# Attention, routed experts and a gated layer on one core: compact attention state, keys transposed in scaled form, two banks for y, ten row buffers, and only the needed zones zeroed

## The chip, the cores and the metric

One core of one Trainium2 chip runs the whole program. The metric is the device time of one launch in microseconds (us). The engines are TensorE (PE in the rows, PEld for its weight loads), VectorE (DVE), ScalarE (ACT), GpSimd (POOL) and SyncE (SP, which issues most transfers).

## The reference, cut to what matters

```python
def _attn_ref(r, k, v, w, u):          # B, H, S, D = 4, 8, 768, 48
    state = zeros((B, H, D, D))
    for t in range(S):
        cur = einsum('bhd,bhe->bhde', u * k[t], v[t])
        y[t] = einsum('bhd,bhde->bhe', r[t], state + cur)
        state = w[:, :, None] * state + einsum('bhd,bhe->bhde', k[t], v[t])

x = y.transpose(0, 2, 1, 3).reshape(3072, 384)
logits = x @ w_gate + modality_bias[modality_id]        # 8 experts
e_idx = argmax(logits); gate_w = softmax(logits)[e_idx]
x = gate_w * (relu(x @ w1[e_idx]) @ w2[e_idx])          # w1 384x1024, w2 1024x384
xn = x / rms(x) * rms_g
out = (silu(xn @ w_gate2) * (xn @ w_val)) @ w_out       # 384 -> 1536 -> 384
```

All data are float32.

## The kernel before, in words

**Attention.** The sequence is cut into 24 tiles of 128 tokens of one batch (tile i: chunk i // 4, batch i % 4), worked on in a software pipeline of steps `s_`. In step s the code issues, in this order:

- `a_state(s-2)`: VectorE adds the state product of tile s-2 (a PSUM bank, `s`) to the state `St` of its batch (L782), GpSimd multiplies the sum by the decay (L784), each in two halves of 64 partitions.
- `a_T(s+1)`, `a_scale(s+1)`: TensorE transposes r and k of the next tile, VectorE scales both transposes by powers of w out of PSUM (L726, `rT` and `kT`).
- `a_load(s+4)`: three loads of 192 KB by SyncE. The rings hold 4 tiles of r, 4 of k and 6 of v.
- `a_A(s)`, `a_mask(s)`: scores on TensorE, the causal copy on VectorE.
- `a_Y(s-1)`: y of tile s-1, from the state (L755) and from the masked scores (L759), in one bank (4), copied out by ScalarE (L762); then the state product (L767).
- `a_diag(s+2)`, `a_rk(s+3)`, `a_kp(s+3)`: products of r, k and u; keys scaled for the state (`kpad`), both on GpSimd; 8 diagonal tiles on ScalarE (L711).
- `hard()`, `send_one()`: routing, and the scatter of one finished tile of x to its experts' rows in `xs` (L242, GpSimd).
- `a_X(s-2)`: gate logits and x of tile s-2 (L656). ScalarE copies x into a buffer of a ring of 6 (L660), GpSimd writes the token number beside it (L661); in the next step VectorE reads the logits (L668).

**Routing.** Every three tiles a route of about 17 small VectorE operations is started. It advances by one operation at each call of `soft()`, which the attention code makes between its own VectorE operations; `hard()` runs what is left up to the rank matmuls (L355, L356, bank 7).

**Experts.** `xs` has for each expert a zone of 800 rows ahead of its tokens, and one dummy zone. A slot is 792 rows of one expert. Slots that are not full read into the zone. `zero_rows` writes zeros to all nine zones during attention (L257, 1.2 MB each, on SyncE's queue, from step 3 to step 19). Two slots known to be full start early, before the last tiles are scattered; the others (two fixed ones, `NFIX`, and more in a loop that is rarely entered) come from a table that is ready at sub-step 9 of the expert phase. The expert phase is a list of sub-steps k of 18 matmuls each (L611, L629 to L631), fed by weight loads of SyncE (L541, L543) through a ring of three chunks.

**The gated layer** follows, from about 455 us on, and is not touched.

Within attention and the expert phase the order of each engine's instructions is that of the code. Every engine works its queue in order, and so does SyncE with its transfers.

Of the kernel before, what the change touches and what calls it, by code (L numbers as in the profile page):

```python
# [18 lines left out]
NP = H // 2  # L19
# [20 lines left out]
XW = DM + 2  # L40
G = 3
EARLY_T = 15
NEARLY = 2
# [13 lines left out]
def moe_chain_kernel(ctx: ExitStack, tc: tile.TileContext, r, k, v, w, u, mod, wgate, mbias,  # L57
# [13 lines left out]
    def bank(n, name=None):  # L71
        return ps.tile([128, 512], F32, tag=f"b{n}", name=name or f"b{n}")
# [19 lines left out]
    def pad_tile(nm, n, pool):  # L92
        if pool is cst:
            t = room[:, 3 * n + "rkv".index(nm), :].rearrange("p (h d) -> p h d", h=H)
        else:
            t = pool.tile([128, H, 64], F32, name=f"{nm}pad{n}")
        pads[nm, n] = t
        P.memset(t[:, :, D:64], 0.0)

# [147 lines left out]
    def body(fast):  # L247
        with ExitStack() as st:
            moe = ExitStack()
            mp = moe.enter_context(tc.tile_pool(name="mp", bufs=2))  # L250
            zrow = {}

            def zero_rows(e):
                if not zrow:
                    zrow[0] = tabs[0:ZONE // 10, KD * HALF:KD * HALF + XW]
                    P.memset(zrow[0], 0.0)
                d = SP.dma_start(out=xs[e * STRIDE:e * STRIDE + ZONE, :].rearrange("(p t) d -> p t d", t=10),  # L257
                                 in_=zrow[0].rearrange("p (t d) -> p t d", t=1).to_broadcast([ZONE // 10, 10, XW]))
                if e < E:
                    tc.declare_no_dep(d.ins, group="xs", reason="rows that no token has")  # L260
                    tc.add_to_no_dep_group("xs", d.ins)

# [49 lines left out]
            def route(g, ls, xt):  # L312
# [39 lines left out]
                yield HARD  # L352
                bk = bank(7, "rank")
                rk = bk[:, 0:G * E]
                T.matmul(rk, tri16, M.rearrange("p g e -> p (g e)"), start=True, stop=False)  # L355
                T.matmul(rk, ones16, C[:, 0:G, :].rearrange("p g e -> p (g e)"), start=False, stop=True)  # L356
                if (g + 1) * G in (EARLY_T, NT):
                    T.matmul(bk[0:1, 128:128 + E], ones16[:, 0:1], C[:, G, :], start=True, stop=True)
                yield SOFT
# [11 lines left out]
                if (g + 1) * G in (EARLY_T, NT):  # L371
                    cnt = p.tile([1, E], F32, name="cntf")
                    V.tensor_copy(cnt, bk[0:1, 128:128 + E])
# [275 lines left out]
            yt, xt, ls = {}, {}, {}  # L649

            def a_X(i):

                yT = yt.pop(i)
                xb = bank(6, "xb")
                for q in range(NP):
                    T.matmul(xb[:, q * SW:(q + 1) * SW], yT[:, q, :], selw[:, q, :], start=True, stop=True)  # L656
                xb3 = xb[:, 0:NP * SW].rearrange("p (q n) -> p q n", q=NP)
                if fast:
                    x = xt[i] = ap.tile([128, XW], F32, name="x", bufs=6)
                    A.activation(x[:, 0:DM].rearrange("p (q n) -> p q n", q=NP), xb3[:, :, 0:2 * D], AF.Copy)  # L660
                    P.tensor_copy(x[:, DM + 1:XW], tokid[:, i:i + 1])  # L661
                g, o = divmod(i, G)
                if o == 0:
                    ls[g] = ap.tile([128, G, E], F32, name="ls", bufs=3)
                return ls[g][:, o, :], xb3[:, :, 2 * D:SW].rearrange("p q e -> p e q")
# [5 lines left out]
            if fast:  # L671
                ac = at.enter_context(tc.tile_pool(name="ac", bufs=1, side="right"))
                kpad = [ac.tile([128, H, 64], F32, name=f"kp{n}") for n in range(5)]
                St = [ac.tile([128, H, 64], F32, name=f"St{b}") for b in range(B)]

# [9 lines left out]
                def padded(nm, i):  # L685
                    return pads[nm, i % ring[nm]]
# [6 lines left out]
                def a_kp(i):  # L693
                    if i < 5:
                        P.memset(kpad[i][:, :, D:64], 0.0)
                    P.tensor_tensor(kpad[i % 5][:, :, 0:D], padded("k", i)[:, :, 0:D], Qt, op=ALU.mult)
                    if i < B:
                        P.memset(St[i], 0.0)

# [46 lines left out]
                def a_Y(i):  # L746
# [16 lines left out]
                    if c < NC - 1:  # L763
                        sb[i] = bank(5, "s")
                        for q in range(NP):
                            for hf in range(2):
                                T.matmul(sb[i][64 * hf:64 * hf + 64, q * D:(q + 1) * D], kpad[i % 5][:, 2 * q + hf, :],  # L767
                                         vv[:, 2 * q + hf, 0:D], start=True, stop=True, skip_group_check=True)

                def a_state(i):  # L770
                    if i in sb:
                        b = i % B
                        sp = sb.pop(i)[:, 0:NP * D].rearrange("p (q d) -> p q d", q=NP)
                        decay = PT[:, :, 128:129].to_broadcast([128, NP, D])
                        for n in range(2):
                            rows = slice(64 * n, 64 * n + 64)
                            sf = St[b].rearrange("p (q two) d -> p two q d", two=2)[rows, n, :, 0:D]
                            if i < B:
                                V.tensor_tensor(sf, sp[rows], decay[rows], op=ALU.mult)
                            else:  # L780
                                tmp = ap.tile([128, NP, D], F32, name=f"stmp{n}")[rows]
                                V.tensor_tensor(tmp, sp[rows], sf, op=ALU.add)  # L782
                                soft()
                                P.tensor_tensor(sf, tmp, decay[rows], op=ALU.mult)  # L784
            else:
                def a_row(i):
                    t = xt[i] = ap.tile([128, XW], F32, name="x", bufs=6)
                    P.tensor_copy(t[:, DM + 1:XW], tokid[:, i:i + 1])
# [18 lines left out]
            with tc.manual_schedule(engines={ET.PE, ET.DVE, ET.Activation, ET.Pool, ET.SP}) if fast else nullcontext():  # L807
# [25 lines left out]
                for s_ in range(0 if fast else -1, NT + 2):  # L833
                    if s_ == 3:
                        zero_rows(E)
                    if 5 <= s_ < 5 + 2 * E and s_ % 2:
                        zero_rows((s_ - 5) // 2)
                    if fast:
# [42 lines left out]
                    if s_ == NT:  # L881
                        for kk in range(KD):
                            slot_x(slots[0], 0, kk, bank((0, 1, 5)[kk], "xtp"))
                    if s_ == 1:
# [85 lines left out]
            for k in range(len(steps) + 1):  # L970
# [52 lines left out]
                if k == NROUTE:  # L1023
# [45 lines left out]
            def overflow():  # L1069
                nonlocal mp, raws1, raws2, xrows  # L1070
                with tc.tile_pool(name="mo", bufs=2) as mp:
                    raws1, raws2, xrows = slot_memory()
                    with tc.For_i(NFIX, ncount, 1) as jv:
                        un = unit_new(slot_new(rt["tabR"], jv), (0, 1))
                        slot_rows(un.s)
                        unit_weights(un, range(1))
# [210 lines left out]
```

## Time and profile before

| | |
|---|---|
| three runs | 914.93, 905.68, 906.70 us; median 906.7 |
| the profiled execution | 903.63 us, span 901.8 us |
| TensorE, VectorE, ScalarE, GpSimd busy | 92%, 53%, 37%, 30% of the span |
| attention | from the start to about 190 us |
| expert phase | first matmul at 195.07 us, to about 445 us |
| gated layer | about 455 us to the end |

Time is read by stage: in the stretch that the change touches, the question is which wait ends last. A line of a view tells when an instruction started, how long it took, and in brackets how long its engine stood idle before it and what ended that.

### The profile page before, as it was taken

Reading aid. Unit: us, or ns where it says so; the run is one execution under the profiler, and the core shown is the slowest. Engines: PE = TensorE matmul, PEld = TensorE weight load, DVE = VectorE, ACT = ScalarE, POOL = GpSimd, SP = SyncE. Lnnn points to the kernel's source line nnn. Section 1 sums busy time; section 2 is a strip of 40 time slices with the busy share of each in tenths; the row PEclk is TensorE's granted clock in tenths of the full one; section 3 lists DMA queues with packets and bytes.
Section 4 is the critical chain, followed back from the end, with each engine's and each line's share of the span. In section 5 each row is a group of like instructions: output and inputs, shape, how many; then the busy total and the mean of one; then the engine's idle time right before and its main releaser. Section 6 shows DMA issues by size and latency. Waiting matters only on the chain.

```text
span 901.8 us, 13427 instructions
## 1 busy us (share of the span) xinstructions
PE 828.4 (92%) x5097; PEld 751.5 (83%) x5097; DVE 478.5 (53%) x969; ACT 332.8 (37%) x731; POOL 267.5 (30%) x314
## 2 busy tenths in 40 slices
PE   6996686988999999999699999999999999999995
PEld 5885576878989899999587888888888888888885
DVE  8985667848565787654178635324423423532121
ACT  3563244554655546543333331231222223122111
POOL 6453445634334234322154430120111013011001
PEclk9998798989999999999899999999999999999998
DMA  9999685275574364560711200110100010000001
GB/s 133 186 210 215 144 207 145 90 193 148 175 243 134 121 203 119 115 113 30 117 54 55 86 36 1 36 36 1 34 28 9 1 36 36 1 1 35 1 1 39
DMA packets 120831, 80.40 MB, mean 89 GB/s; under 512 B 85142, under 2 KB 111534, under 8 KB 120750
## 3 DMA queue, kind: packets, MB, share of 16 engines
q1 hardware_dynamic: 117470, 69.91, 32.6%
q0 software_dynamic: 3072, 9.46, 2.9%
q8 instruction: 43, 0.70, 0.4%
q14 instruction: 38, 0.31, 0.2%
q10 hardware_dynamic: 208, 0.00, 0.0%
HBM read 53.91 MB, written 25.46 MB: 88 GB/s over the span
## 4 chain that ended last, share of the span: by engine, by line
PE 53%; DMA 13%; issue 13%; DVE 10%; ACT 5%; POOL 4%; SPq 0%; POOLq 0%; ACTq 0%; DVEq 0%
PE vb L1116 11%; PE gb L1116 11%; PE hp L611 8%; DMA xs<-x,pos_all 7%; PE ob L1131 4%; PE ob L1132 4%; PE ob L1130 4%; PE y L630 2%; PE y L631 2%; PE y L629 2%; DMA kpad<-k 1%; DMA raw<-moe_w_gate 1%; DVE w1l L53 1%; DVE Am L743 1%; PE xb L656 1%
## 5 line engine op out<-in xcount | busy, mean ns | idle before, releaser
L1120 DVE TENSOR_TENSOR sg<-sg,vb 128x512 f32<-128x512 f32 x72 | 49.5, 687 | 216.8 <-PE vb L1116 211.7
L1130 PE MATMUL ob<-woh,acth 128*128 128x384 f32 x288 | 97.7, 339 | 6.5 <-ACT woh L285 6.5
L1131 PE MATMUL ob<-wol,acth 128*128 128x384 f32 x288 | 98.2, 341 | 2.6 <-POOL wol L53 2.5
L1122 ACT ACTIVATE acth<-sg 128x512 fp32r<-128x512 f32 x72 | 45.5, 632 | 148.6 <-DVE sg L1120 148.6
L1132 PE MATMUL ob<-woh,actl 128*128 128x384 f32 x288 | 97.7, 339 | 0.0
L1119 ACT ACTIVATE sg<-gb 128x512 f32<-128x512 f32 x72 | 42.8, 595 | 132.3 <-PE gb L1116 132.3
L711 ACT ACTIVATE Am<-ident,cd 128x128 f32<-128x128 f32 x184 | 56.4, 389 | 53.4 <-DVE cd L704 53.4
L611 PE MATMUL hp<-xh,w1h 128*128 128x396 f32 x192 | 68.5, 357 | 3.8 <-DVE hl L616 2.2
L242 POOL DMA_INDIRECT out<-room,toks x24 | 23.2, 966 | 155.1 <-ACT room L1141 84.3
L611 PE MATMUL hp<-xh,w1l 128*128 128x396 f32 x192 | 66.5, 346 | 2.4 <-DVE w1l L53 2.4
L611 PE MATMUL hp<-xl,w1h 128*128 128x396 f32 x192 | 66.2, 345 | 0.2 <-DVE xl L584 0.2
L630 PE MATMUL y<-hl,w2h 128*128 128x396 f32 x192 | 65.6, 342 | 0.8 <-DVE hl L616 0.8
L629 PE MATMUL y<-hh,w2h 128*128 128x396 f32 x192 | 65.6, 341 | 0.3 <-ACT hh L614 0.3
L631 PE MATMUL y<-hh,w2l 128*128 128x396 f32 x192 | 65.7, 342 | 0.0
L53 DVE TENSOR_TENSOR actl<-sg,acth 128x512 fp32r<-128x512 f32 x60 | 41.5, 692 | 41.9 <-ACT acth L1122 41.9
L1130 PEld LDWEIGHTS ob<-woh,acth 128*128 128x128 f32 x288 | 54.6, 190 | 10.0 <-ACT woh L285 7.1
L1131 PEld LDWEIGHTS ob<-wol,acth 128*128 128x128 f32 x288 | 54.4, 189 | 7.7 <-POOL wol L53 5.3
L616 DVE SCALAR_TENSOR_TENSOR hl<-hp,hh 128x396 fp32r<-128x396 f32 x64 | 36.2, 566 | 40.5 <-ACT hh L614 40.5
L1132 PEld LDWEIGHTS ob<-woh,actl 128*128 128x128 f32 x288 | 54.5, 189 | 0.1
L614 ACT ACTIVATE hh<-hp 128x396 fp32r<-128x396 f32 x64 | 32.0, 499 | 44.8 <-PE hp L611 44.5
L656 PEld LDWEIGHTS xb<-tabs,yT 128*128 128x128 f32 x192 | 27.2, 217 | 24.1 <-DVE ls L668 12.8
L1116 PE MATMUL gb<-xh,wgh 128*128 128x512 f32 x108 | 42.5, 394 | 1.9 <-issue 1.9
(258 smaller groups left out, 2114.7 us busy)
## 6 DMA issues: line engine op xcount, KB each, us to landing
xs<-tabs SPq DMA_DIRECT2D x9, 1206.2 KB
room<-moe_w SPq DMA_DIRECT2D x26, 384.0 KB
raw<-moe_w SPq DMA_DIRECT2D x14, 384.0 KB
xslot<-xs SPq DMA_DIRECT2D x8, 597.1 KB
raw<-moe_w_gate SPq DMA_DIRECT2D x12, 384.0 KB
raw<-moe_w_val SPq DMA_DIRECT2D x12, 384.0 KB
z<-ys SPq DMA_DIRECT2D x6, 768.0 KB
raw<-moe_w_out SPq DMA_DIRECT2D x12, 384.0 KB
```

The lines of the kernel that those rows point to most:

```text
L53: eng.tensor_tensor(out, a, h.bitcast(F32), op=ALU.subtract)
L611: T.matmul(hp[:, 0:HALF], l[:, kk, :], m[:, kk], start=(n == 0), stop=(n == 8))
L629: T.matmul(y, bh[:, sl], hh, start=(f == 0), stop=False)
L630: T.matmul(y, bh[:, sl], hl, start=False, stop=False)
L631: T.matmul(y, bl[:, sl], hh, start=False, stop=(f == NFE - 1))
L711: A.activation(am[i][:, h % 2, h // 2, :], ident, AF.Copy, scale=c_[:, h:h + 1])
L1116: T.matmul(dst, l, m[:, kk], start=(n == 0), stop=(n == 8))
L1120: V.tensor_tensor(sg, sg, vb, op=ALU.mult)
L1122: A.activation(ah, sg, AF.Copy)
L1130: T.matmul(ob[o][:, 0:DM], ah[:, sl], wo_h[f], start=(f == 0), stop=False)
L1131: T.matmul(ob[o][:, 0:DM], ah[:, sl], wo_l[f], start=False, stop=False)
L1132: T.matmul(ob[o][:, 0:DM], al[:, sl], wo_h[f], start=False, stop=(f == NF2 - 1))
```

## The change

- `St` is [128, 4, 64] in place of [128, 8, 64] with empty halves: the two heads of a pair lie on partitions 0 to 63 and 64 to 127. The update of the state is one VectorE and one GpSimd operation over 128 partitions in place of two each over 64. The state part of y is 8 matmuls of 64 rows by 64 columns in place of 4 of 128 by 128.
- From tile 2 on, the key's transpose is made of `kpad`, which is scaled already; ScalarE copies it out of PSUM in place of VectorE's product.
- y has banks 4 and 7 in turn. The rank matmuls move to bank 5, which now also holds two state products in turn.
- x has a ring of 10 buffers in place of 6.
- The dummy zone is zeroed as before; of the others, one for each of the two fixed slots, after the table is ready (and one in the rare loop).
- `soft()` is called twice less in a step, so more of a route runs in `hard()`.

```diff
+XB = 10
 ...
+            def zero_zone(sl):
+                SP.dma_start(out=xs[0:E * STRIDE, :].rearrange("(e n) d -> e n d", e=E)[bass.ds(sl.e, 1), 0:ZONE, :]
+                             .rearrange("o (p t) d -> p (o t) d", t=10), in_=zsrc)
 ...
-                bk = bank(7, "rank")
-                rk = bk[:, 0:G * E]
+                rk = aux[:, A_RK:A_RK + G * E]
 ...
+            aux = bank(5, "aux")
 ...
-                    x = xt[i] = ap.tile([128, XW], F32, name="x", bufs=6)
+                    x = xt[i] = ap.tile([128, XW], F32, name="x", bufs=XB)
 ...
-                St = [ac.tile([128, H, 64], F32, name=f"St{b}") for b in range(B)]
+                St = [ac.tile([128, NP, 64], F32, name=f"St{b}") for b in range(B)]
 ...
+                        src = padded(nm, i) if nm == "r" or i < 2 else kpad[i % 5]
                         for q in range(NP):
-                            T.transpose(tb[:, q * 128:(q + 1) * 128], pair(padded(nm, i), q), ident)
+                            T.transpose(tb[:, q * 128:(q + 1) * 128], pair(src, q), ident)
 ...
-                        V.tensor_tensor(t, tb.rearrange("p (q n) -> p q n", q=NP), tab, op=ALU.mult)
                         tr[i].append(t)
-                        soft()
+                        if nm == "kT" and i >= 2:
+                            A.activation(t.rearrange("p q n -> p (q n)"), tb, AF.Copy)
+                        else:
+                            V.tensor_tensor(t, tb.rearrange("p (q n) -> p q n", q=NP), tab, op=ALU.mult)
+                            soft()
 ...
-                    y = bank(4, "y")
+                    y = bank(7 if i % 2 else 4, "y")
                     if c:
                         for q in range(NP):
-                            T.matmul(y[:, q * 128:(q + 1) * 128], pair(St[b], q), rT[:, q, :],
-                                     start=(q == 0), stop=False, skip_group_check=True)
+                            for hf in range(2):
+                                sl = slice(64 * hf, 64 * hf + 64)
+                                T.matmul(y[sl, q * 128:(q + 1) * 128], St[b][sl, q, :], rT[sl, q, :],
+                                         start=(q == 0), stop=False, skip_group_check=True)
 ...
-                        sb[i] = bank(5, "s")
+                        sb[i] = aux[:, i % 2 * NP * D:(i % 2 + 1) * NP * D]
 ...
-                        for n in range(2):
-                            rows = slice(64 * n, 64 * n + 64)
-                            sf = St[b].rearrange("p (q two) d -> p two q d", two=2)[rows, n, :, 0:D]
 ...
-                                tmp = ap.tile([128, NP, D], F32, name=f"stmp{n}")[rows]
-                                V.tensor_tensor(tmp, sp[rows], sf, op=ALU.add)
-                                soft()
-                                P.tensor_tensor(sf, tmp, decay[rows], op=ALU.mult)
+                            tmp = ap.tile([128, NP, D], F32, name="stmp")
+                            V.tensor_tensor(tmp, sp, sf, op=ALU.add)
+                            soft()
+                            P.tensor_tensor(sf, tmp, decay, op=ALU.mult)
 ...
                     if s_ == 3:
-                        zero_rows(E)
-                    if 5 <= s_ < 5 + 2 * E and s_ % 2:
-                        zero_rows((s_ - 5) // 2)
+                        zero_row()
+                        zero_dummy()
 ...
                     for j in range(NFIX):
                         slots.append(slot_new(rt["tabR"], j))
+                        zero_zone(slots[-1])
```

The order of instructions on GpSimd changes as follows, at the first scatters of attention. The rows stand in the order of the engine's queue, with what each waits for in brackets; DMASW0 is the semaphore on which the first scatter signals that it has landed, DMASW1 the second. Before:

```order
L242 DMA xs_63<-x_469,pos_all_168 31776x386 [waits DVE_49,Activation_49]
L661 COPY x_919<-tokid_166 128x1
L784 TENSOR_TENSOR St2_193<-stmp0_922,power_74 64x4x48 [waits DVE_49]
L784 TENSOR_TENSOR St2_193<-stmp1_925,power_74 64x4x48 [waits DMASW0_49,DVE_49,Pool_49]
L690 TENSOR_TENSOR dg_994<-rpad3_203,kpad3_205 128x384 [waits DMAHW5_49,DMAHW4_49,Pool_49]
L696 TENSOR_TENSOR kp1_187<-kpad3_205,tabs_92 128x8x48 [waits PE_49]
L242 DMA xs_63<-x_549,pos_all_168 31776x386 [waits Activation_49]
L661 COPY x_1004<-tokid_166 128x1
```

And of the change, the first scatter, and then the place five scatters later at which its landing is first waited for:

```order
L244 DMA xs_63<-x_465,pos_all_168 31776x386 [waits DVE_49,Activation_49,Pool_49]
L670 COPY x_910<-tokid_166 128x1
L798 TENSOR_TENSOR St2_194<-stmp_913,power_74 128x4x48 [waits DVE_49]
L699 TENSOR_TENSOR dg_985<-rpad3_203,kpad3_205 128x384 [waits DMAHW3_49,DMAHW2_49]
L705 TENSOR_TENSOR kp1_188<-kpad3_205,tabs_92 128x8x48 [waits PE_49,Pool_49]
```

```order
L244 DMA xs_63<-x_910,pos_all_168 31776x386 [waits Activation_49]
L670 COPY x_1388<-tokid_166 128x1 [waits DMASW0_49]
L798 TENSOR_TENSOR St3_195<-stmp_1391,power_74 128x4x48 [waits DVE_49,Pool_49]
L699 TENSOR_TENSOR dg_1469<-room_73 128x384 [waits DMAHW4_49,DMAHW3_49]
L705 TENSOR_TENSOR kp1_188<-room_73,tabs_92 128x8x48 [waits PE_49]
```

The wait for a scatter moved from the state update right behind it to the buffer of x that is reused ten tiles on, and one state update of two is gone.

On SyncE the two zone writes come in the expert phase, behind the loads of the table's registers (`tabfb`) and ahead of the next chunk of weights. Before:

```order
L526 TENSOR_LOAD tabfb_2755 [waits DVE_49]
L526 ISA x2
L526 TENSOR_LOAD tabfb_2755
L526 ISA x2
L541 ISA
L541 DMA room_73<-moe_w1 128x3x256 [waits DMAHW0_49,DVE_49]
L643 DMA ys_64<-tabs_92 128x3x396 [waits DMAHW1_49,DVE_49,Activation_49]
L543 ISA
L543 DMA room_73<-moe_w2 128x2x384 [waits DMAHW2_49,Pool_49]
```

Of the change:

```order
L264 ISA
L264 DMA xs_63<-tabs_92 800x1x386 [waits DMAHW2_49,DMAHW3_49,DMAHW0_49,DMASW7_49]
L648 DMA ys_64<-tabs_92 128x3x396 [waits DMAHW1_49,DVE_49,Activation_49]
L531 TENSOR_LOAD tabfb_2746
L531 ISA x2
L264 ISA
L264 DMA xs_63<-tabs_92 800x1x386 [waits DMAHW0_49]
L546 ISA
L546 DMA room_73<-moe_w1 128x3x256
L548 ISA
L548 DMA room_73<-moe_w2 128x2x384 [waits DMAHW4_49,Pool_49]
```

Each zone write now stands behind the load of its slot's register, and the chunk of weights, the next in the queue before, behind both. The second write waits for the first (DMAHW0), and the first for the last scatter (DMASW7). The rows marked ISA compute registers.

## Rows read from the trace of the kernel before

**Rows 1.** Busy us of PE, PEld, DVE, ACT, POOL; granted clock, DMA share, GB/s

```profile
40.00:58.00 18.00, 16.98 (x222) 15.51 (x218) 17.10 (x52) 11.79 (x37) 10.01 (x15) 1.00 0.98 209
58.00:173.00 115.00, 86.92 (x954) 78.99 (x951) 76.26 (x213) 44.49 (x135) 58.23 (x82) 0.85 0.73 170
...
101.00:107.00 6.00, 2.33 (x12) 2.26 (x12) 4.95 (x18) 1.84 (x6) 4.34 (x6) 0.50 0.27 69
```

**Rows 2.** Timeline of PE, line L755: start us, us, instruction

```profile
40.07 1.16 PE L755 MATMUL y<-rT,St 128*128 128x128 f32 x8
...
58.08 1.16 PE L755 MATMUL y<-rT,St 128*128 128x128 f32 x8
...
63.67 1.16 PE L755 MATMUL y<-rT,St 128*128 128x128 f32 x8
...
161.17 1.19 PE L755 MATMUL y<-rT,St 128*128 128x128 f32 x8
```

**Rows 3.** Waits of POOL and ACT, 56 to 190 us: total us, times, longest

```profile
POOL St L784 <- DMA xs<-x,pos_all: 42.8, 9, 9.1
...
ACT x L660 <- DMA xs<-x,pos_all: 29.6, 9, 7.5
...
POOL St L784 <- DMA kpad<-k: 7.0, 1, 7.0
```

**Rows 4.** Timelines of POOL, ACT and DVE around one scatter, 90 to 102 us

```profile
90.59 1.16 POOL L242 DMA_INDIRECT xs<-x,pos_all  x1 [0.15 <-issue]
...
101.52 0.51 POOL L784 TENSOR_TENSOR St<-stmp,power 64x192 f32<-64x192 f32 x1 [9.10 <-DMA xs<-x,pos_all]
...
101.46 0.49 ACT L660 ACTIVATE x<-xb 128x384 f32<-128x384 f32 x1 [7.54 <-DMA xs<-x,pos_all]
...
101.98 0.19 DVE L668 TENSOR_REDUCE ls<-xb 128x8 f32<-128x32 f32 x1 [7.84 <-ACT x L660]
```

**Rows 5.** Timeline of PE, one undisturbed step and the rank matmul ahead of it

```profile
49.45 0.17 PE L356 MATMUL rank<-C,ones 128*128 128x24 bf16 x1 [1.02 <-DVE C L342]
...
52.48 1.16 PE L755 MATMUL y<-rT,St 128*128 128x128 f32 x8
53.57 1.09 PE L759 MATMUL y<-Am,room 128*64 128x128 f32 x16
```

**Rows 6.** Lines by form, 0 to 215 us: count, busy us, mean ns of one

```profile
L726 DVE TENSOR_TENSOR kT<-kTp,power 128x512 f32<-128x512 f32 x24 | 16.4, 682 | 0.2
...
L762 ACT ACTIVATE yT<-y 128x512 f32<-128x512 f32 x24 | 14.2, 591 | 20.7 <-PE s L767 14.8 <-PE y L759 5.7
...
L782 DVE TENSOR_TENSOR stmp<-s,St 64x192 f32<-64x192 f32 x32 | 11.2, 350 | 0.8 <-PE s L767 0.2
```

**Rows 7.** Timeline of PE: two score matmuls of 64 rows, one row group

```profile
166.03 0.27 PE L736 MATMUL Aa<-rT,kT 64*128 64x128 f32 x1
...
166.14 0.27 PE L736 MATMUL Aa<-rT,kT 64*128 64x128 f32 x1
```

**Rows 8.** Window as in rows 1 (loads alone), landing of scatters, zone writes (page, part 6)

```profile
25.00:30.00 5.00, 5.00 (x78) 4.66 (x76) 4.90 (x11) 3.06 (x10) 3.55 (x5) 1.00 1.49 166
...
DMA to landing us min/median/max: 2.6/5.0/10.8
...
xs<-tabs SPq DMA_DIRECT2D x9, 1206.2 KB
```

**Rows 9.** Timelines of POOL, ACT and PE at the end of attention

```profile
176.06 1.11 POOL L242 DMA_INDIRECT xs<-x,pos_all  x1 [0.28 <-POOL St L784]
...
185.95 2.12 ACT L560 ACTIVATE xslot<-xslot 99x384 f32<-99x384 f32 x4
...
195.07 0.70 PE L611 MATMUL hp<-xh,w1h 128*128 128x396 f32 x1 [0.54 <-DVE xl L584]
```

**Rows 10.** Timelines of SP and ACT: a chunk of weights, issued and first used

```profile
229.50 0.37 SPq L541 DMA_DIRECT2D room<-moe_w  x1
...
245.29 0.52 ACT L591 ACTIVATE w1h<-room 128x384 fp32r<-128x384 f32 x1
```

More of the change, by code (lines that the diff above doesn't have):

```diff
@@ L97, in pad_tile @@
         pads[nm, n] = t
-        P.memset(t[:, :, D:64], 0.0)
+        if nm != "k" or n < 2:
+            P.memset(t[:, :, D:64], 0.0)
     def a_load(i, names="rkv"):
@@ L250, in body, with zero_row, zero_dummy @@
             mp = moe.enter_context(tc.tile_pool(name="mp", bufs=2))
[L251 to L261, printed above, removed]
+            zrow = tabs[0:ZONE // 10, KD * HALF:KD * HALF + XW]
+            zsrc = zrow.rearrange("p (t d) -> p t d", t=1).to_broadcast([ZONE // 10, 10, XW])
+            def zero_row():
+                P.memset(zrow, 0.0)
+            def zero_dummy():
+                SP.dma_start(out=xs[DUMMY:DUMMY + ZONE, :].rearrange("(p t) d -> p t d", t=10), in_=zsrc)
+            def zero_zone(sl):
+                SP.dma_start(out=xs[0:E * STRIDE, :].rearrange("(e n) d -> e n d", e=E)[bass.ds(sl.e, 1), 0:ZONE, :]
+                             .rearrange("o (p t) d -> p (o t) d", t=10), in_=zsrc)
             def dec_load(src, n):
@@ L352, in route @@
                 yield HARD
-                bk = bank(7, "rank")
-                rk = bk[:, 0:G * E]
-                T.matmul(rk, tri16, M.rearrange("p g e -> p (g e)"), start=True, stop=False)
-                T.matmul(rk, ones16, C[:, 0:G, :].rearrange("p g e -> p (g e)"), start=False, stop=True)
+                rk = aux[:, A_RK:A_RK + G * E]
+                T.matmul(rk, tri16, M.rearrange("p g e -> p (g e)"), start=True, stop=False, skip_group_check=True)
+                T.matmul(rk, ones16, C[:, 0:G, :].rearrange("p g e -> p (g e)"), start=False, stop=True,
+                         skip_group_check=True)
                 if (g + 1) * G in (EARLY_T, NT):
-                    T.matmul(bk[0:1, 128:128 + E], ones16[:, 0:1], C[:, G, :], start=True, stop=True)
+                    T.matmul(aux[0:1, A_CNT:A_CNT + E], ones16[:, 0:1], C[:, G, :], start=True, stop=True,
+                             skip_group_check=True)
                 yield SOFT
@@ L649, in body @@
             yt, xt, ls = {}, {}, {}
+            aux = bank(5, "aux")
+            A_RK, A_CNT = 2 * NP * D, 2 * NP * D + G * E
             def a_X(i):
@@ L697, in a_kp @@
                     if i < B:
-                        P.memset(St[i], 0.0)
+                        P.memset(St[i][:, :, D:64], 0.0)
                 def a_diag(i, dg):
@@ L772, in a_state @@
                         b = i % B
-                        sp = sb.pop(i)[:, 0:NP * D].rearrange("p (q d) -> p q d", q=NP)
+                        sp = sb.pop(i).rearrange("p (q d) -> p q d", q=NP)
                         decay = PT[:, :, 128:129].to_broadcast([128, NP, D])
-                        for n in range(2):
-                            rows = slice(64 * n, 64 * n + 64)
-                            sf = St[b].rearrange("p (q two) d -> p two q d", two=2)[rows, n, :, 0:D]
-                            if i < B:
-                                V.tensor_tensor(sf, sp[rows], decay[rows], op=ALU.mult)
-                            else:
-                                tmp = ap.tile([128, NP, D], F32, name=f"stmp{n}")[rows]
-                                V.tensor_tensor(tmp, sp[rows], sf, op=ALU.add)
-                                soft()
-                                P.tensor_tensor(sf, tmp, decay[rows], op=ALU.mult)
+                        sf = St[b][:, :, 0:D]
+                        if i < B:
+                            V.tensor_tensor(sf, sp, decay, op=ALU.mult)
+                        else:
+                            tmp = ap.tile([128, NP, D], F32, name="stmp")
+                            V.tensor_tensor(tmp, sp, sf, op=ALU.add)
+                            soft()
+                            P.tensor_tensor(sf, tmp, decay, op=ALU.mult)
             else:
                 def a_row(i):
-                    t = xt[i] = ap.tile([128, XW], F32, name="x", bufs=6)
+                    t = xt[i] = ap.tile([128, XW], F32, name="x", bufs=XB)
                     P.tensor_copy(t[:, DM + 1:XW], tokid[:, i:i + 1])
@@ L882, in body @@
                         for kk in range(KD):
-                            slot_x(slots[0], 0, kk, bank((0, 1, 5)[kk], "xtp"))
+                            slot_x(slots[0], 0, kk, bank((0, 1, 2)[kk], "xtp"))
                     if s_ == 1:
@@ L1072, in overflow @@
                     raws1, raws2, xrows = slot_memory()
+                    zero_row()
                     with tc.For_i(NFIX, ncount, 1) as jv:
                         un = unit_new(slot_new(rt["tabR"], jv), (0, 1))
+                        zero_zone(un.s)
                         slot_rows(un.s)
```

2 lines of the change are left out of this document (1 added, 1 removed).

## The prediction

> **What bounds the kernel now.** I read the busy time by stretch first. Between 40 and 58 us [rows 1] TensorE is busy 16.98 us of 18 and VectorE 17.10 of 18, at a granted clock of 1.00: nothing stands still. From 58 to 173 us TensorE is busy only 86.92 of 115 us, and the clock averages 0.85. So the question is what each step of attention waits for after 58 us.
>
> The timeline of the state part of y gives the length of a step [rows 2]. y of tile 4 starts at 40.07 and of tile 7 at 58.08: 18.01 / 3 = 6.00 us a step. Tile 8 starts at 63.67 and tile 18 at 161.17: 97.5 us for ten steps, 9.75 each. The ten long steps are thus 97.5 - 10 x 6.00 = 37.5 us too long.
>
> The waits of that stretch name the cause [rows 3]. GpSimd's state update waits 42.8 us in nine places for the landing of a scatter of x, and ScalarE's copy of x 29.6 us in nine places. One such place [rows 4]: a scatter is issued at 90.59. The state update, which follows it in GpSimd's queue, idles 9.10 us; the copy of x on ScalarE idles 7.54 us and starts at 101.46; the logits on VectorE, which read the same bank, idle 7.84 us and start at 101.98. The scores' copies, the state's sum and the routing stand behind them on VectorE, so TensorE has nothing to do. The order on GpSimd shows why: the second half of the state update waits for DMASW0, the landing of the scatter issued two rows above. The token of the next tile is to be written into the buffer that this scatter reads (the ring holds 6), and the program puts that wait on the instruction ahead.
>
> **The change, part by part.** The sum is made against the profiled execution, 903.6 us, which is 3.1 below the median of the three runs (906.7).
>
> *Ten buffers of x.* In the new order the landing of the first scatter is first waited for five scatters later. At 6.0 us a step that is 30 us, where landings took 2.6 to 10.8 us [rows 8]. The ten long steps fall to 6.00: **-37.5**. Late next is what sets an undisturbed step. Of such a step [rows 5], 5.60 us pass from one y to the next when TensorE has work, and every third step has a wait of 1.02 us for the rank matmul, with some issue besides. I take the measured mean, 6.00; the bounds are 5.5 (the dense step less 0.1 from the edit on y) and 6.25 (lost covers of two engines, below). That is -42.5 to -35.
>
> *Zone writes.* Nine of 1206 KB go away from attention, but for one [rows 8]. They compete with the three loads of a step, 3 x 192 KB = 590 kB in bytes. Loads alone moved 166 GB/s with the queues full: 3.6 us of a 6.0 us step. With a scatter of 198 kB (1.2 us at that rate) it is 4.8 of 6.0. The load share fits without the zone writes, and they are a reason for the scatters' slow landings. Priced at nothing beyond the cadence above.
>
> *Key transposes from* `kpad`*, copied by ScalarE.* VectorE loses 682 ns a step; ScalarE gains a copy of the same shape as yT, 591 ns [rows 6]. ScalarE is busy 11.79 of 18 us in three steps, so 3.9 of 6.0 becomes 4.5: covered. If that cover is gone (the copy late for the scores), a step pays at most 0.59; I take 0. *One state update of 128 rows* in place of two of 64: VectorE loses 350 ns more, GpSimd one operation of 0.51 [rows 4]. VectorE falls from 5.7 to 4.7 us a step. It was as full as TensorE, so where steps were bound by it this gains. That was so at the start (4.90 us of 5.00 between 25 and 30 us, [rows 8]), in few steps: **-1** (0 to -2).
>
> *The state part of y in 64-row passes.* Before, 8 passes in 1.09 us [rows 5]. After, 16 passes. Two 64-row matmuls of the scores start 0.11 us apart, each 0.27 long [rows 7]. If the two heads of a pair run side by side, the eight pairs take 8 x 0.11 = 0.9 us; if in series, 16 x 0.11 = 1.8. So -0.2 to +0.7 a step for 20 steps, -4 to +13. The scores write their two heads to two banks, the new y writes both to one, on different partitions; no row shows that. I take the end nearest to the scores' row, and count it as 0. The Trainium skill, "TensorEngine Tiling (Array Packing)", section "Restrictions and Gotchas", says that different row tiles cannot access the same PSUM bank at the same time. By that rule the pairs go in series and the sum is 13 higher.
>
> *Fewer* `soft()`*.* Two calls less a step are six operations of a route less under cover, in three steps. At the 0.19 us of a small VectorE operation [rows 4] that is up to 1.1 us a route, which the rank matmul may wait for; five routes run in the stretch, so 0 to +5.5. VectorE also has a microsecond a step less to do, so I take **+1**. The two banks of y and the two halves of bank 5 take waits away from TensorE and add one of the state's sum behind a rank matmul of 0.17 us [rows 5]: 0.
>
> *The end of attention.* Scatter 14 is issued at 176.06, ScalarE's work on the first early slot starts at 185.95, the first expert matmul at 195.07 [rows 9]. In the new order that ScalarE work stands one place earlier against the last copies of y; if its gather is late by as much as the cadence gained, the last tiles wait. **+1** (0 to +4).
>
> *Two zone writes in the expert phase.* They stand ahead of a chunk of weights that was issued at 229.50 and first used at 245.29 [rows 10], 15.8 us later. At 209 GB/s, the rate of the stretch from 40 to 58 us [rows 1], a write of 1.2 MB takes 5.9 us, and the second waits for the first. Some 6 us of this delay the chunk's issue, and it then shares the transfer with the second write, 6 more, beside its own transfer of 393 kB, about 2. Together 14 of 15.8 us: just covered. Late next, if not, is the first matmul of that chunk. **+0.5** (0 to +8).
>
> Sum: -37.5 - 1 + 1 + 1 + 0.5 = -36.0, and 903.6 - 36.0 = 867.6, so 868.
>
> **The rivals.**
> - *Passes in series.* +13 gives 881. For it: two row groups into one bank, which before never did. Against: they lie on different partitions. Were it so, dense steps would be 0.7 longer.
> - *Another wait takes the scatters' place: loads.* GpSimd waited 7.0 us once for `kpad` [rows 3], though the zone writes were the likely reason. At 4.8 of 6.0 us of transfer a step, two thirds of the rate (107 GB/s) makes that 7.5. Ten steps x 1.5 = 15: 883.
> - *VectorE was the true bound of the 6.00.* It was busy 17.10 of 18 us. With 1.03 us a step less, TensorE's dense 5.5 remains: 13 steps from tile 8 on x 0.5 = 6.5, and some at the start: 860.
> - *The change doesn't do it.* The nine waits for scatters move from GpSimd's state update to its token copy, as long as before. Then only the smaller terms are left: 900 to 905. Against: the order puts 30 us between scatter and wait.
> - *The other side: the granted clock.* Where attention runs dense without the stalls, TensorE could be held at 1.2 GHz, its lower level. At 0.50, as from 101 to 107 us behind a stall [rows 1], a dense step of 5.6 us costs 5.6 more; the 37 us are gone at seven such steps, and ten give about 922. Against: between 40 and 58 us the same dense steps had 1.00 throughout [rows 1], and the mean of 0.85 fell where the engine idled.
>
> **How the numbers follow.** Chances: the forecast 0.60 (868, its own range 862 to 874 from the bounds of the tail, the routes and the chunk); series 0.12 (881); loads 0.12 (883); VectorE the bound 0.08 (860); no effect 0.04; the clock 0.04. The range from 859 to 884 takes in the first four and leaves out 0.08 and a tail of the forecast's own terms. One per cent is 9 us, about what a measurement of this kernel can tell from no change. The first four cases are faster by more, 0.92; no effect is within it, 0.04; the clock gives slower, 0.04.
>
> **What would show it.** Right: no wait of GpSimd or ScalarE for a scatter between 56 and 160 us; y of successive tiles 6.0 us apart from tile 4 on; the granted clock at 1.00 from 40 to 150 us; the first expert matmul at about 158 us in place of 195; the key copy on ScalarE at 0.59 us; two of the 16 passes starting within 0.11 us, with the next line of y 0.9 us behind; no wait of ScalarE for the chunk behind the zone writes. Wrong: y to its masked part 1.8 us (series); GpSimd or ScalarE waiting for `kpad`, r or v (loads); steps of 5.5 us (VectorE was the bound); a clock near 0.5 in dense steps; a stall of the first expert matmul or after the second zone write. What would make the forecast wrong as a whole is a cadence other than 6.0: a tenth of a microsecond a step is 1.3 us.

## The result and the profile after

The changed kernel takes 878.5 us (median of four runs, 877.5 to 879.9), the kernel before on the same chip 910.2 us: a ratio of 0.966 (95% interval 0.961 to 0.971). The forecast was 868 us in a range of 859 to 884. The time is inside the range and 10 us above the forecast; the medians differ by 31.7 us, where 36 were forecast. The profiled execution took 877.53 us (span 875.8): 26.0 us of span less than before. The profiled execution of the kernel before (903.63 us) was 6.6 us quicker than the median of its timings, so the balance by stage below shows 26.0 us of the 31.7.

The busy time by stretch (us of PE, PEld, DVE, ACT, POOL; granted clock, DMA share, GB/s), to set beside [rows 1]:

```profile
40.00:58.00 18.00, 17.78 (x240) 16.12 (x238) 13.42 (x41) 11.76 (x34) 8.00 (x13) 0.92 0.73 138
58.00:150.00 92.00, 88.26 (x1233) 79.24 (x1231) 67.79 (x221) 62.81 (x179) 55.23 (x75) 0.98 0.67 156
```

TensorE is now busy 88.26 of 92 us behind 58 us, at a clock of 0.98; before, the same 92 us held 68.60 us of its work. VectorE fell from 17.10 to 13.42 of 18 us between 40 and 58 us. The waits of GpSimd and ScalarE for scatters ([rows 3]: 42.8 and 29.6 us) are gone from the list; the longest of GpSimd there is now a scatter that waits for its positions (total us, times, longest; the second line is the longest of ScalarE):

```profile
POOL xs L244 <- DVE pos_all L373: 21.4, 2, 12.7
ACT yT L778 <- PE aux L783: 16.0, 9, 2.3
```

These are idle times of GpSimd and ScalarE. The longest wait of TensorE between 56 and 158 us is 1.74 us, of a rank matmul for the route's work on VectorE. The timeline of TensorE (start us, us) at the start of y of tiles 4 (with the next line of y), 8, 18, 20 and 21, and the first expert matmul:

```profile
44.62 1.09 PE L771 MATMUL y<-rT,St 64*64 64x128 f32 x16
45.64 1.09 PE L775 MATMUL y<-Am,vpad 128*64 128x128 f32 x16
...
67.14 1.09 PE L771 MATMUL y<-rT,St 64*64 64x128 f32 x16
...
124.71 1.09 PE L771 MATMUL y<-rT,St 64*64 64x128 f32 x16
...
135.77 1.09 PE L771 MATMUL y<-rT,St 64*64 64x128 f32 x16
...
145.20 1.09 PE L771 MATMUL y<-rT,St 64*64 64x128 f32 x16
...
160.09 0.45 PE L616 MATMUL hp<-xh,w1h 128*128 128x396 f32 x1 [1.08 <-DVE xl L589]
```

Tile 8 to tile 18 takes 57.57 us in place of 97.5 [rows 2]. The balance by stage, against the same marks of before:

| stage | before | after | difference | term of the forecast |
|---|---|---|---|---|
| start to y of tile 4 | 40.07 | 44.62 | +4.6 | -1 with the start |
| tile 4 to tile 8 | 23.60 | 22.52 | -1.1 | 0 |
| tile 8 to tile 18 | 97.50 | 57.57 | -39.9 | -37.5, with +1 for `soft()` |
| tile 18 to the first expert matmul | 33.90 | 35.38 | +1.5 | +1 |
| first expert matmul to the end of the span | 706.7 | 715.7 | +9.0 | +0.5 |
| sum | 901.8 | 875.8 | -26.0 | -36 |

The size of the main term held and was a little larger. Two places gave back what was not foreseen: 4.6 us at the start, 9.0 us from the first expert matmul on. Of the 9.0 us, 6.6 lie before the last expert matmul (237.6 us after the first, 231.0 before), and the rest behind it, ahead of the gated layer's first output matmul, which now waits 7.6 us for its weights in place of 6.5.

**The start.** Tile 3 is the first whose y lies in bank 7. TensorE and VectorE there:

```profile
38.53 1.29 PE L775 MATMUL y<-Am,vpad 128*64 128x128 f32 x16 [4.27 <-DVE mT L228]
```

```profile
38.31 0.17 DVE L228 COPY mT<-mps 128x24 f32<-128x24 f32 x1
```

A small transpose for the gate's bias (`mps`, L225) also uses bank 7. Its only reader, the copy mT, is issued a step later on VectorE, behind that step's scores and products, so y of tile 3 waits 4.27 us for an operation of 0.17 us. Before, y had bank 4 alone and nothing waited for mT. Behind this wait the granted clock is 0.70 from 38.5 to 40.5 us and 0.50 from 40.5 to 42.5: the matmuls of x take 2.04 us there and 1.14 one step later.

**The expert phase.** SyncE's queue, the two zone writes and the chunk of weights behind them:

```profile
191.40 0.71 SPq L264 DMA_DIRECT2D xs<-tabs  x1
...
200.74 0.63 SPq L264 DMA_DIRECT2D xs<-tabs  x1
201.58 0.48 SPq L546 DMA_DIRECT2D room<-moe_w  x1
```

The second write was issued 9.3 us after the first, for whose landing it waits, and the chunk 10.2 us after the first. Before, it was issued at 229.50 [rows 10], 34.4 us after the first expert matmul; now 41.5 us after it. ScalarE, which converts the weights, then waits for several of them (idle time in brackets; the first row is the chunk behind the zone writes, the other two are weights of the gated layer), and TensorE waits for what stands behind the conversion on ScalarE:

```profile
210.79 0.53 ACT L596 ACTIVATE w1h<-room 128x384 fp32r<-128x384 f32 x1 [2.08 <-DMA room<-moe_w]
...
239.41 0.56 ACT L279 ACTIVATE da<-raw 128x384 f32<-128x384 f32 x1 [5.07 <-DMA raw<-moe_w_val]
...
364.17 0.55 ACT L279 ACTIVATE da<-raw 128x384 f32<-128x384 f32 x1 [6.46 <-DMA raw<-moe_w_gate]
```

```profile
212.44 0.45 PE L616 MATMUL hp<-xh,w1h 128*128 128x396 f32 x1 [1.08 <-DVE hl L621]
...
365.99 0.45 PE L634 MATMUL y<-hh,w2h 128*128 128x396 f32 x1 [2.75 <-ACT hh L619]
```

At the place of the last row the kernel before waited 0.30 us. The wait of ScalarE ahead of it is not new, though; before, it was 4.35 us:

```profile
394.12 0.56 ACT L275 ACTIVATE da<-raw 128x384 f32<-128x384 f32 x1 [4.35 <-DMA raw<-moe_w_gate]
```

Up to the last expert matmul ScalarE waits 15.5 us for weights in all, 5.1 before. The chunk itself was nearly in time: its first use is 50.7 us after the first expert matmul, 50.2 before.

### The profile page after: what moved, and what is told of

Read it like the earlier page. It is cut to its first block, busy times and chain, and to the rows that moved or that the text cites. A ratio compares the mean times of both kernels' runs of the same rounds, so it can differ in the third digit from the quotient of the medians.

```text
span 875.8 us, 13683 instructions
## 1 busy us (share of the span) xinstructions
PE 820.1 (94%) x5257; PEld 742.7 (85%) x5257; DVE 451.7 (52%) x927; ACT 342.1 (39%) x753; POOL 257.4 (29%) x296
## 4 chain that ended last, share of the span: by engine, by line
PE 35%; issue 11%; DVE 3%; POOL 1%; DMA 1%; ACT 1%; POOLq 0%; DVEq 0%
PE gb L1132 12%; PE vb L1132 12%; PE ob L1147 4%; PE ob L1148 4%; PE ob L1146 4%; DMA raw<-moe_w_out 1%; DVE da L283 1%; POOL out L244 1%; DVE sg L1136 0%; POOL wol L54 0%; DVE da L285 0%; DVE da L287 0%; ACT da L279 0%; POOL xl2b L54 0%; DVE n L946 0%
## 5 line engine op out<-in xcount | busy, mean ns | idle before, releaser
L1135 ACT ACTIVATE sg<-gb 128x512 f32<-128x512 f32 x72 | 42.8, 594 | 132.2 <-PE gb L1132 132.2
L54 DVE TENSOR_TENSOR actl<-sg,acth 128x512 fp32r<-128x512 f32 x60 | 41.5, 692 | 41.9 <-ACT acth L1138 41.9
L621 DVE SCALAR_TENSOR_TENSOR hl<-hp,hh 128x396 fp32r<-128x396 f32 x64 | 36.2, 565 | 38.5 <-ACT hh L619 38.4
L1132 PE MATMUL gb<-xl,wgh 128*128 128x512 f32 x108 | 43.2, 400 | 0.0
```

The costliest lines, as they stand in the source:

```text
L1132: T.matmul(dst, l, m[:, kk], start=(n == 0), stop=(n == 8))
L1135: A.activation(sg, gb, AF.Silu)
```

## The experiments

All ratios are to runs of the kernel before on the same chip, with 95% intervals. The ranges of the expectations were set from the 878.5 us above. On the chips of these runs the kernel before took 902.6 to 904.2 us and not 910.2, so a ratio of 0.966, that of the changed kernel, stands here for 872 to 874 us; no time is to be set against 878.5. The forecast named the ring of six buffers as the cause of the waits for scatters, and priced the zone writes at nothing. The first group tests that.

**Ten buffers alone, in the kernel before.**

```diff
-                    x = xt[i] = ap.tile([128, XW], F32, name="x", bufs=6)
+                    x = xt[i] = ap.tile([128, XW], F32, name="x", bufs=10)
```

> The kernel before with ten buffers of x and nothing else. The order of GpSimd's instructions shows that the second half of each state update still waits for the scatter just issued, although no buffer is reused so early. Theory A (the forecast's: the ring of six is the cause of both waits): the ten long steps fall from 9.75 to about 6.0 us, the kernel to about 870 us. Theory B (GpSimd's wait comes from the state update in two halves and alone sets the long steps): no gain, 903 to 912 us, ScalarE's copy of x without a wait, GpSimd's wait still about 40 us in all. Theory C (either of the two waits holds a step by itself): as B, within 10 us of before.

898.1 us against 903.7, ratio 0.995 (0.991 to 0.998). ScalarE no longer waits for scatters; GpSimd's state update does (waits, 56 to 190 us):

```profile
POOL St L784 <- DMA xs<-x,pos_all: 36.6, 10, 7.6
```

Theory A falls; B and C are not told apart by it. The ring did not cause GpSimd's wait. With ten buffers the second half of the state update waits already behind the first two scatters, issued at 56.30 and 63.52 us: 2.02 us at 60.48 and 5.97 us at 71.18, where no buffer of the ring is reused yet. So the forecast's cause was wrong: the wait belongs to the update in two halves. Why the program gives the second half that wait, no run shows.

**Six buffers in the changed kernel** (`XB = 6`).

> The changed kernel with a ring of six buffers of x. ScalarE's copy of x and GpSimd's token copy then wait for the scatter of one step earlier. Theory A: the stalls come back, 905 to 915 us. Theory B: little is lost, 878 to 885 us. Theory C: most of the stalls come back, 895 to 910 us.

872.9 us, ratio 0.966 (0.960 to 0.972), as the changed kernel. Theory A falls a second time: without the zone writes in attention the ring of ten is worth nothing that can be measured.

**The state update of the changed kernel in two halves on GpSimd.**

```diff
-                            P.tensor_tensor(sf, tmp, decay, op=ALU.mult)
+                            for n in range(2):
+                                rows = slice(64 * n, 64 * n + 64)
+                                P.tensor_tensor(sf[rows], tmp[rows], decay[rows], op=ALU.mult)
```

> The changed kernel with ten buffers, but GpSimd's state update split in two halves of 64 partitions again; the second half then waits for the scatter just issued. Theory A: 878 to 882 us (some 0.4 us more on GpSimd a step, covered). Theory B and C: the long steps come back, 900 to 912 us, with a wait of GpSimd's state update for scatters of 30 us or more.

881.8 us, ratio 0.978 (0.972 to 0.984): some 10 us are lost of the gain, not 30. The time lies in the range of theory A, but by the ratio that theory asked for no loss, and none of the theories stated fits. The first expert matmul starts at 170.5 us, 10.4 later than in the changed kernel. The wait is back in the trace, but it is short:

```profile
POOL St L801 <- DMA xs<-x,pos_all: 8.9, 6, 2.2
```

The scatters now land sooner, so there is less to wait for. That pointed to the zone writes.

**The kernel before with the late zone writes** of the changed kernel, and nothing else (the dummy zone stays in attention).

```diff
-                    if 5 <= s_ < 5 + 2 * E and s_ % 2:
-                        zero_rows((s_ - 5) // 2)
 ...
                         slots.append(slot_new(rt["tabR"], j))
+                        zero_zone(slots[-1])
```

> The kernel before (ring of six, state update in halves) with the zone writes of the changed kernel: the dummy zone in attention, two after the table. Theory D (the landings were slow because of the zone writes, and both waits are long only for that): GpSimd's wait for scatters falls from 42.8 us to 20 or less, ScalarE's from 29.6 to a few, and the kernel comes to 880 to 890 us. Theory C (each wait holds the step whatever the zone writes do): 898 to 906 us.

879.4 us against 902.6 (median of four, of which one took 889.6), ratio 0.978 (0.971 to 0.984): theory D, 0.6 us below its range. GpSimd's state update waits little for scatters, and ScalarE's copy not at all; the token copy waits 11.8 us in two places:

```profile
POOL St L786 <- DMA xs<-x,pos_all: 5.3, 4, 1.6
```

With six buffers and the update in halves, two thirds of the gain are there. Not all of it need be the landings: the wait of 7.0 us for a load of k [rows 3] is gone as well. The landings of scatters issued between 50 and 160 us (min, median, max), in the kernel before, in this one, and in the changed kernel:

```profile
DMA to landing us min/median/max: 2.7/6.2/10.8
```

```profile
DMA to landing us min/median/max: 2.7/3.4/7.9
```

```profile
DMA to landing us min/median/max: 3.1/3.2/3.3
```

**The changed kernel with all zones zeroed in attention**, as before, and none late.

```diff
                         zero_dummy()
+                    if 5 <= s_ < 5 + 2 * E and s_ % 2:
+                        zero_rows((s_ - 5) // 2)
 ...
-                        zero_zone(slots[-1])
```

> The changed kernel with all zones zeroed in attention, as before, and none behind the table. If the new order alone shields attention from slow landings: y of successive tiles stays 5.5 to 6.0 us apart, the expert phase gets back about 8 us, 866 to 872 us. If the zone writes also make the loads of r, k and v late (theory D, wider): steps grow by 1 to 2 us for some ten steps, 880 to 895 us.

870.7 us, ratio 0.965 (0.962 to 0.968), not told apart from the changed kernel. The landings are slow again, and attention loses little (first expert matmul at 162.12 us, 2.0 later than in the changed kernel):

```profile
DMA to landing us min/median/max: 3.6/6.3/9.8
```

Up to the last tiles nothing waits for them. The loads of k do come later: GpSimd's products wait 10.2 us for them in all, and tile 8 to tile 18 takes 61.7 us in place of 57.57, 9.5 of them in one step. So the two repairs cover one another. The next run puts both causes back into the changed kernel and keeps everything else.

**All zones in attention, and GpSimd's update in halves** (the two diffs above).

> The changed kernel with all zones zeroed in attention and GpSimd's state update split in halves: slow landings together with an instruction that waits for the scatter just issued. Theory E (the long steps need both; each of the two repairs alone removes most of them): the long steps come back, 890 to 902 us, GpSimd's state update waiting 30 us or more for scatters. Rival (each part is worth a fixed amount, whatever the other is): early zones gave about -1 us and the halves about +9 against the changed kernel, so 878 to 883 us.

901.4 us, ratio 0.998 (0.995 to 1.001): the whole gain is gone, with ten buffers, the wide VectorE sum, ScalarE's copy of kT and two banks of y all in place. Theory E holds, and fixed prices for each part are excluded. Tile 8 to tile 18 takes 85.4 us (57.57 in the changed kernel, 97.5 before). GpSimd's timeline shows one place:

```profile
86.17 1.17 POOL L244 DMA_INDIRECT xs<-x,pos_all  x1 [0.15 <-issue]
87.35 0.19 POOL L676 COPY x<-tokid 128x1 f32<-128x1 f32 x1
87.49 0.51 POOL L807 TENSOR_TENSOR St<-stmp,power 64x192 f32<-64x192 f32 x1
94.53 0.51 POOL L807 TENSOR_TENSOR St<-stmp,power 64x192 f32<-64x192 f32 x1 [6.53 <-DMA xs<-x,pos_all]
```

The first half runs at once, the second 6.53 us later, when the scatter has landed. The products of r and k and the scaled keys of the next tiles stand behind it. TensorE then waits for the route's work on VectorE:

```profile
98.35 0.18 PE L365 MATMUL aux<-C,ones 128*128 128x24 bf16 x1 [6.31 <-DVE C L352]
```

This is a stall like that of [rows 4]. The expected 30 us of waits were not found as such: the view puts 20.3 us down to scatters, in seven places. Further long idle times of the same second halves (6.0 to 7.1 us in three places) it puts down to TensorE, for which the order shown ahead of the prediction has no wait, so these too are probably waits for scatters.

**All zones in attention, and six buffers.**

> The changed kernel with all zones zeroed in attention and a ring of six buffers of x. GpSimd's token copy and ScalarE's copy of x then wait for the scatter of one step earlier, whose landing takes about 6 us with the zone writes. If a step's distance (5.5 us) hides most of it: 870 to 880 us. If the ring is a cause of the long steps beside the halves: 885 to 900 us.

876.2 us, ratio 0.969 (0.964 to 0.974), first expert matmul at 168.92 us. GpSimd's token copy waits for the scatter of one step earlier:

```profile
POOL x L676 <- DMA xs<-x,pos_all: 25.0, 9, 4.6
```

A step's distance hides most of a slow landing. In the trace the ring of ten saves 6.8 us of attention here; in the whole time the intervals of the two kernels meet.

The four corners, with ten buffers or six as marked:

| | zones in attention | zones late |
|---|---|---|
| update in halves | before with ten buffers 0.995; changed kernel with both 0.998 | before, six buffers 0.978; changed kernel, ten 0.978 |
| update whole | 0.965 (ten), 0.969 (six) | 0.966 (ten), 0.966 (six) |

The second group tests what else the forecast priced, and the two givebacks.

**The copy of kT on VectorE.**

```diff
-                            A.activation(t.rearrange("p q n -> p (q n)"), tb, AF.Copy)
+                            V.tensor_copy(t.rearrange("p q n -> p (q n)"), tb)
```

> The changed kernel with the copy of the key's transpose on VectorE in place of ScalarE (some 0.6 us a step). If VectorE bound the steps before: steps of 5.53 us grow towards 6.0, some 0.4 us for 20 steps, 882 to 890 us. If VectorE has room in the changed kernel: 876 to 880 us.

876.1 us, ratio 0.969 (0.966 to 0.973), not told apart from the changed kernel by time. In the trace the dense steps stay at 5.53 us; every third step, with the rank matmuls, takes 6.5 to 6.8 us in place of 6.0 to 6.3 (tile 8 to tile 18: 59.67 us against 57.57), and the first expert matmul starts 4.1 us later. So VectorE's work lengthens the step of a route and, in this kernel, no other.

**One bank for y** (`bank(4, "y")` for all tiles).

> The changed kernel with y always in bank 4. The wait of 4.3 us of tile 3 for the copy mT goes, since y no longer shares bank 7 with it. If the second bank hides the copy of y out of PSUM: TensorE waits for ScalarE in each step, 0.5 us or more for 20 steps, 882 to 895 us. If that copy has ended anyway by the next y, 5 us later: 872 to 876 us.

871.5 us, ratio 0.964 (0.961 to 0.968). The wait for mT is gone (y of tile 4 starts at 39.10), but most of it is lost two steps on, as in the next run, and the first expert matmul starts at 159.62, 0.5 us earlier than in the changed kernel. Dense steps stay at 5.53, so the second bank of y hides nothing that the trace shows: that copy out of PSUM has evidently ended before the next y.

**mT one step earlier.**

```diff
         T.transpose(mps[:, 0:NT], mf, ident[0:NT, 0:NT])
-        yield
         mT = pool.tile([128, NT], F32, name="mT")
         V.tensor_copy(mT, mps[:, 0:NT])
+        yield
```

> The changed kernel with one VectorE copy (mT) one step earlier, behind the transpose it reads. In the changed kernel y of tile 3 has bank 7 and waits 4.3 us for that copy. Theory: that wait goes and the attention's later parts move up by it, 873 to 875 us. Rival: the same VectorE work is ahead of the masked scores anyway, or the time is lost again before the experts: 877 to 879 us.

870.1 us, ratio 0.964 (0.958 to 0.970). y of tile 4 starts at 38.16, 6.5 us earlier, but part is lost two steps on:

```profile
38.16 1.09 PE L771 MATMUL y<-rT,St 64*64 64x128 f32 x16
...
47.67 0.17 PE L358 MATMUL aux<-M,tri 128*128 128x24 bf16 x1 [1.42 <-DVE C L340]
48.81 0.17 PE L359 MATMUL aux<-C,ones 128*128 128x24 bf16 x1 [0.96 <-DVE C L346]
```

```profile
48.00:54.00 6.00, 5.19 (x43) 4.74 (x44) 3.46 (x17) 3.42 (x10) 2.43 (x3) 0.72 0.66 130
```

The first route's rank matmuls wait 1.42 and 0.96 us for VectorE, probably because more of the route is left to its end now, and the granted clock from 48 to 54 us is 0.72. At the first expert matmul 3.1 us are left (157.03 against 160.09). By time the run is not told apart from the changed kernel; the gain of 3 us is that of the trace.

**Both givebacks at once: zones in attention, mT early.**

> The changed kernel with all zones zeroed in attention and the copy mT one step earlier: both givebacks removed. Expected 865 to 868 us if the two add up (3 us at the start, 7 to 9 us in the expert phase less 2 us in attention); 869 to 871 us if the steps take the start's gain back.

875.1 us, ratio 0.968 (0.964 to 0.971): a miss. The two do not add up. GpSimd's products now wait for keys:

```profile
POOL dg L705 <- DMA kpad<-k: 12.0, 3, 4.6
POOL dg L705 <- DMA room<-k: 10.2, 3, 4.8
```

These are loads of k, with the zone writes beside them; in the run with the zones in attention alone the same two rows held 10.2 us together. y of tile 4 starts 7 us earlier here (38.27 against 45.22), so the loads probably had less of a lead; that was not tried apart.

**mT early, and the second late zone write behind the gather of the first fixed slot.**

```diff
-                        zero_zone(slots[-1])
+                        if j == 0:
+                            zero_zone(slots[-1])
 ...
                     slot_rows(nxt)
+                    if n == 2:
+                        zero_zone(slots[3])
```

> The changed kernel with the copy mT one step earlier and the second late zone write moved behind the gather of the first fixed slot, so that the next chunk of weights no longer stands behind two zone writes on SyncE. If that queue place is what the expert phase loses: 864 to 868 us. If the transfers themselves are the loss: 869 to 872 us.

869.1 us, ratio 0.962 (0.958 to 0.965), the lowest of all; its interval meets that of the changed kernel and that of mT early alone (0.958 to 0.970), so the time decides between neither expectation. The chunk is now issued 4.5 us behind the first zone write, not 10.2:

```profile
190.28 0.72 SPq L264 DMA_DIRECT2D xs<-tabs  x1
...
194.78 0.46 SPq L546 DMA_DIRECT2D room<-moe_w  x1
```

From the first expert matmul to the end of the span it takes 710.0 us, against 712.5 with mT early alone and 715.7 in the changed kernel: in the traces the queue place is worth some 2.5 us.

## Why the prediction was right or wrong

- **The place of the loss and its size: right.** The ten long steps were the loss, and they fell to the length of undisturbed ones: 57.57 us for ten steps, 5.76 each, inside the bounds of 5.5 to 6.25. Some of it is below 6.00 because a step with a rank matmul now takes 6.0 to 6.3 us in place of 6.8, and a dense one 5.53 in place of 5.60.
- **The cause: wrong, and the main term came out by luck.** The step that failed is "the token of the next tile is to be written into the buffer that this scatter reads (the ring holds 6), and the program puts that wait on the instruction ahead". The wait stands on the second half of the state update, and it stands there still with ten buffers, where no token copy needs it: the part that was priced at -37.5 gave 0.5% alone. The ring caused ScalarE's wait and one of 3.9 us of the token copy. What removed GpSimd's wait is the state update as one operation, which the forecast priced as VectorE's 350 ns and one GpSimd operation of 0.51 us. So the wait did not move to the reused buffer, as is said ahead of the prediction; these are two waits, and each part of the change removes its own.
- **The zone writes "priced at nothing beyond the cadence": wrong.** Taken alone out of attention they gave 2.2%. With them a scatter landed in 6.2 us, without in 3.4. The sentence that they are "a reason for the scatters' slow landings" was there, and no price was drawn from it. That the sum came out is due to two repairs of the same stall, neither of which was priced for it: either is worth 2 to 3.5% alone, both together 3.4%.
- **The start, -1: wrong sign, +4.6.** The edit on y's banks was put at 0 because it "takes waits away". The forecast did not ask which other tile had bank 7; the transpose of the bias had it, and y of tile 3 waited 4.27 us for its copy.
- **The zone writes in the expert phase, +0.5 (0 to +8): right for the chunk, the loss larger.** The write took 9.3 us until the second could be issued, against 5.9 from the rate of another stretch. The chunk behind them was still nearly in time: ScalarE waits 2.08 us for it and TensorE 1.08, where the forecast's sign was no wait. The other 8 us of the 9.0 lie elsewhere. About half of them stand behind later weights: TensorE waits 1.8 us at 241 us, and 3.8 at 366 us where 1.1 before. How much of that is these writes stays open. From the first to the last expert matmul it took 230.9 to 231.7 us in four traces without late writes, but 233.1 and 235.0 in two more; with both late writes as in the changed kernel it took 236.6 to 238.1 us in four traces, where the first expert matmul starts at 157 to 160 us, but 232.3 to 234.5 in three, where it starts at 164 to 171 us. So the early start may have its part; that was not tried apart. By time, taking the late writes out gave nothing clear of the noise (0.965 against 0.966).
- **The end of attention, +1: right**, +1.5. `soft()`**, +1: not needed.** The rank matmuls waited 0.27 to 0.34 us for VectorE in the four routes between 58 and 125 us, less than the 1.02 us of [rows 5].
- **The rivals.** Passes in series: excluded. The 16 passes of y's state part are followed by the next line 1.02 us later (44.62 to 45.64), 0.13 for a pair; in series they would take 1.8. By the rule of the Trainium skill, "TensorEngine Tiling (Array Packing)", section "Restrictions and Gotchas", that different row tiles cannot access the same PSUM bank at the same time, they should have gone in series; this trace does not agree where the two write different partitions of the bank. Loads as the next wait: not in the changed kernel, but seen with the zones in attention (10.2 us of GpSimd for k, and 22.2 with mT early). Two thirds of 166 GB/s are 111 and not 107, so the price of that rival should have been 880 us. VectorE as the bound: true of the steps with a route; dense steps changed by 0.07 us only. The clock: 0.98 from 58 to 150 us, so the rival is excluded there; 0.92 from 40 to 58 us, where the sign was 1.00, is the short fall behind the wait for mT.

## What to carry to other kernels

When an instruction waits for a transfer, read in the order which dependence puts the wait there before naming a buffer; a change that removes the wait by another part will look like a confirmation. A stall can need two things, a slow transfer and an instruction right behind it, and then the parts of a change are not to be added: test them at the corners. When a PSUM bank gets a new use, list every tile that has it, those used once included, and see how late their readers run.

## What the runs showed of the hardware

The 16 passes of 64 rows by 64 columns, of two row groups that write different partitions of one PSUM bank, took 1.02 us, 0.13 us a pair; one after the other they would take 1.8 by the 0.11 us of [rows 7]. With writes of 1.2 MB among the transfers the median landing of a 198 KB scatter was 6.3 us against 3.2 without them in the changed kernel, and 6.2 against 3.4 in the kernel before. Whether it is the common destination `xs` or the load on the transfers that does it, no run shows. Behind a wait of TensorE of 4.27 us the granted clock fell to 0.50, its lower level, for 2 us.
